# A second Strassen level over pairs of blocks, with PSUM banks copied to PSUM banks

## The chip, the core and the metric

The kernel runs on one core of a Trainium2 chip. A core has a matrix engine (TensorE, PE in the profile, with its weight loads as PEld), three other compute engines (VectorE = DVE, ScalarE = ACT, GpSimd = POOL), a queue of DMA issues on SyncE (SP), another one on GpSimd, and 16 DMA engines that serve both queues. Operands lie in SBUF, TensorE writes its products to one of eight PSUM banks of 128 x 512 fp32 numbers. Each engine takes its instructions in order; between engines semaphores make one wait for another. The metric is the device time of one execution in microseconds (us), as the median over runs.

## The reference

```python
x = A_x                                        # 1 x 2048 x 640
g = sigmoid((x * gate_w).sum(-1, keepdims=True))
a = real part of DFT over the sequence of the DFT over the hidden axis of x
b = (gelu(x @ w_gate) * (x @ w_up)) @ w_down   # F = 1728 hidden features
return g * a + (1 - g) * b
```

Everything is fp32. The change touches only `x @ w_gate` and `x @ w_up` and what feeds them.

## The kernel before

**Numbers.** fp32 products are made of three matmuls in a faster fp32 form (`mm3`, lines 84 to 87): each operand is split into a high part (a ScalarE copy, `high`, line 74) and a low part (a VectorE subtraction, `low`, line 77), and high x high, high x low and low x high are added up in one PSUM bank. So each operand of TensorE costs one ScalarE and one VectorE instruction, unless the split is already there.

**Stages.** First a prologue loads x and computes the first block of hidden features and the 64 that remain at the end; then twelve chunks compute gate and up for 128 features each (f = 1 to 12), from about 48 to 348 us; then come the down product (from 348 to about 500 us), the DFT over the sequence, and the last stage. The hidden values go to DRAM (`hA`, `hT`, by GpSimd's queue) and come back for the down product.

**A chunk.** For each of two token pairs (tp = 0, 1; 1024 tokens each) `gate_up` takes the weights as a 2 x 2 matrix A (gate and up by the two halves of inner blocks 0 to 3) and the tokens as a 2 x 2 matrix B, and uses the seven products of the Strassen-Winograd scheme: A11·B11, S1·T1, S2·T2, A12·B21, S3·T3, S4·B22, A22·T4. Each product is two `mm3` (two inner blocks i); the fifth inner block is added with `g5`, `u5` and `D`. That makes 18 `mm3`, 54 matmuls, per chunk and token pair, and 108 matmuls per chunk. Intermediate sums stay in the banks X, Z and V, and ScalarE copies X to SBUF as s1 and s2 on the way (L131 of the profile).

**Weights.** `load_w(f)` loads the two raw tiles wa and wb of chunk f, makes the sums S1 to S4 (`ws`) and the difference D (`wd`) on VectorE, and splits all of them. It is called a whole chunk ahead. Its raw tiles, parts and most other tiles of 4 KB per partition share one pool of 48 slots (tag "s4"); a new tile waits until the slot's former tile has been read for the last time. At the end of each chunk stand the sums of the down weights or up weights for later stages (`sum_wd`, `sum_wu`, lines 344 to 366: two loads, four VectorE sums, a store; for three of the up weights also negations `un` on ScalarE) and two of sixteen pieces of the gate's row sum (`load_z`, lines 386 to 391: a load, a multiply by the gate's weights and a reduction on VectorE).

**What sets the order.** In the prologue and from the down product on, the order of the engines is that of the code. In the chunks in between it is a scheduler's: it decides from priorities and from when operands are ready which instruction an engine takes next. Each engine then keeps to that list on the chip. The rows of such lists are shown below, with their line in the kernel; the last number behind an underscore only tells tiles apart.

## Time and profile before

| | |
|---|---|
| median of 3 runs | 1032.38 us (1030.0 to 1032.62) |
| the profiled execution | 1031.27 us, its span on the core 1029.5 us |
| TensorE busy | 1023.9 us, 99%, 4530 matmuls recorded |
| VectorE busy | 770.6 us, 75%, 1030 instructions |
| ScalarE busy | 449.6 us, 44%, 570 instructions |
| GpSimd busy | 132.2 us, 13% |
| read from and written to HBM | 169.21 MB, 63.98 MB |

The span runs from the first to the last instruction on the core; the execution's own time also has what lies around it. A matmul's row shows 0.39 us, yet the next one starts 0.23 us after it, because matmuls are pipelined: for TensorE, distances between starts tell the cost. Nearly all of a VectorE or ScalarE instruction's time is its own. In rows of waits, the three numbers are the us in total, how often, and the longest.

### The profile page before, as it was taken

How to read it: one execution, taken by the hardware profiler on the slowest of the kernel's cores; microseconds unless marked ns; L12 is line 12 of the kernel's file. 1: busy time of each engine (PE TensorE's matmuls, PEld its weight loads, DVE VectorE, ACT ScalarE, POOL GpSimd, SP SyncE). 2: the span in 40 equal slices, each digit the busy share in tenths (PEclk: the TensorE clock that was granted, in tenths of full speed). 3: DMA queues.
4: the chain of work that ended last, by engine and by line, in shares of the span. 5: the costliest groups of instructions: out<-in, count | busy, mean ns of one | idle time of the engine just before them, and what ended most of it. 6: DMA issues, size and time to landing. Idle time of an engine off the chain costs nothing.

```text
span 1029.5 us, 12790 instructions
## 1 busy us (share of the span) xinstructions
PE 1023.9 (99%) x4530; PEld 846.2 (82%) x4530; DVE 770.6 (75%) x1030; ACT 449.6 (44%) x570; POOL 132.2 (13%) x237
## 2 busy tenths in 40 slices
PE   9999999999999999999999999999999999999998
PEld 7888888888888888888888888888888888888887
DVE  6998675767654967986798975796678769697775
ACT  5453334343523546556345443343344344365430
POOL 0012121212121200100010011002000200021013
PEclk9999999999999999999999999999999999999999
DMA  8246644746446997878866577557656878897748
GB/s 299 74 153 219 221 169 160 239 160 240 154 148 215 381 346 242 276 253 287 288 216 206 209 224 280 178 198 245 257 177 217 273 275 278 288 328 212 283 94 133
DMA packets 78609, 234.05 MB, mean 227 GB/s; under 512 B 10096, under 2 KB 18320, under 8 KB 78544
## 3 DMA queue, kind: packets, MB, share of 16 engines
q1 hardware_dynamic: 57968, 169.31, 48.6%
q0 software_dynamic: 20432, 63.73, 18.4%
q8 instruction: 35, 0.57, 0.2%
q14 instruction: 30, 0.25, 0.1%
q10 hardware_dynamic: 144, 0.20, 0.1%
HBM read 169.21 MB, written 63.98 MB: 227 GB/s over the span
## 4 chain that ended last, share of the span: by engine, by line
PE 98%; DMA 1%; DVE 0%; ACT 0%; issue 0%; SPq 0%; ACTq 0%
PE pX L85 8%; PE pX L86 8%; PE pX L87 8%; PE pZ L86 5%; PE pZ L85 5%; PE pZ L87 5%; PE pV L86 3%; PE pV L85 3%; PE pV L87 3%; PE pL L85 3%; PE pL L87 3%; PE pL L86 3%; PE pY L87 1%; PE pY L85 1%; PE pR L87 1%; PE pR L85 1%
## 5 line engine op out<-in xcount | busy, mean ns | idle before, releaser
L74 ACT ACTIVATE ch<-csa 128x1024 fp32r<-128x1024 f32 x32 | 34.0, 1063 | 88.4 <-DVE csa L436 53.4
L131 ACT ACTIVATE s<-pX 128x512 f32<-128x512 f32 x64 | 37.8, 596 | 77.2 <-PE pX L87 69.2
L74 ACT ACTIVATE ch<-cra 128x1024 fp32r<-128x1024 f32 x32 | 33.9, 1058 | 47.4 <-PE pL L86 21.6
L77 DVE TENSOR_TENSOR cl<-crb,ch 128x1024 fp32r<-128x1024 f32 x32 | 39.1, 1221 | 17.0 <-ACT ch L74 9.7
L77 DVE TENSOR_TENSOR cl<-cra,ch 128x1024 fp32r<-128x1024 f32 x32 | 39.1, 1222 | 15.5 <-ACT ch L74 15.1
L86 PE MATMUL pL<-cl,xah 128*128 128x512 f32 x128 | 49.8, 389 | 0.0
L87 PE MATMUL pL<-ch,xal 128*128 128x512 f32 x128 | 49.8, 389 | 0.0
L85 PE MATMUL pL<-ch,xah 128*128 128x512 f32 x128 | 49.3, 389 | 0.0
L226 POOL DMA_DIRECT2D hA<-s x48 | 26.1, 544 | 177.0 <-DVE s L313 170.6
L303 DVE TENSOR_TENSOR s<-s,pV 128x512 f32<-128x512 f32 x24 | 16.3, 683 | 41.8 <-PE pV L87 17.6
L77 DVE TENSOR_TENSOR cl<-csb,ch 128x1024 fp32r<-128x1024 f32 x32 | 39.2, 1224 | 6.3 <-ACT ch L74 4.7
L74 ACT ACTIVATE ch<-crb 128x1024 fp32r<-128x1024 f32 x32 | 33.8, 1055 | 21.0 <-DVE cl L77 7.8
L77 DVE TENSOR_TENSOR cl<-csa,ch 128x1024 fp32r<-128x1024 f32 x32 | 39.1, 1221 | 4.0 <-ACT ch L74 3.3
L74 ACT ACTIVATE ch<-csb 128x1024 fp32r<-128x1024 f32 x32 | 33.9, 1059 | 11.9 <-PE pL L86 6.9
L77 DVE TENSOR_TENSOR kl<-kw,kh 128x1024 fp32r<-128x1024 f32 (+1 forms) x26 | 31.4, 1208 | 10.0 <-ACT kh L74 10.0
L74 ACT ACTIVATE kh<-kw 128x1024 fp32r<-128x1024 f32 (+1 forms) x26 | 27.3, 1048 | 11.6 <-DMA kw<-wsd 7.3
L312 ACT ACTIVATE s<-s 128x512 f32<-128x512 f32 x24 | 15.2, 633 | 38.8 <-DVE s L311 38.8
L788 POOL DMA_DIRECT2D uA<-s x16 | 8.7, 542 | 159.3 <-DVE s L834 152.5
L87 PEld LDWEIGHTS pL<-ch,xal 128*128 128x128 f32 x128 | 24.0, 188 | 5.0
L86 PEld LDWEIGHTS pL<-cl,xah 128*128 128x128 f32 x128 | 24.0, 188 | 5.0
L85 PEld LDWEIGHTS pL<-ch,xah 128*128 128x128 f32 x128 | 24.0, 188 | 5.0
L226 POOL DMA_DIRECT2D hT<-s x48 | 26.0, 543 | 14.9 <-DVE s L317 3.9
(3584 smaller groups left out, 3332.6 us busy)
## 6 DMA issues: line engine op xcount, KB each, us to landing
cra<-in_ct SPq DMA_DIRECT2D x64, 512.0 KB, 3.9
crb<-in_ct SPq DMA_DIRECT2D x64, 512.0 KB, 4.8
hA<-s POOLq DMA_DIRECT2D x48, 256.0 KB, 4.7
hT<-s POOLq DMA_DIRECT2D x48, 256.0 KB, 4.8
kr<-hA SPq DMA_DIRECT2D x24, 512.0 KB, 7.8
kr<-hT SPq DMA_DIRECT2D x24, 512.0 KB, 6.5
ux<-uA SPq DMA_DIRECT2D x24, 512.0 KB, 5.5
ux<-uT SPq DMA_DIRECT2D x16, 512.0 KB, 7.1
```

The costliest lines, as they stand in the source:

```text
L74: nc.scalar.activation(hi, raw, AF.Copy)
L77: nc.vector.tensor_tensor(lo, raw, hi.bitcast(F32), op=ALU.subtract)
L85: nc.tensor.matmul(ps, lh, rh, start=first, stop=False, skip_group_check=True)
L86: nc.tensor.matmul(ps, lh, rl, start=False, stop=False, skip_group_check=True)
L87: nc.tensor.matmul(ps, ll, rh, start=False, stop=last, skip_group_check=True)
L131: nc.scalar.activation(m, src, AF.Copy)
L226: nc.gpsimd.dma_start(to[:, i], src)
L303: tt(s1, s1, V, op=ALU.add)
L312: nc.scalar.activation(s2, s2, AF.Gelu_apprx_tanh)
L788: nc.gpsimd.dma_start(to[:, i], src)
```

## The change

Chunks 1 and 2 stay as they are. Chunks 3 to 12 are taken in five pairs (p = 1 to 5, f = 2p + 1 and 2p + 2). In a pair, A11·B11 for the two chunks and the two token pairs is itself a 2 x 2 by 2 x 2 product: rows are the two chunks, the inner dimension the two inner blocks, columns the two token pairs. So is A12·B21. `pair_first` computes each of the two (J = 1 for A11·B11, J = 2 for A12·B21) by a second level of the same scheme, 7 `mm3` in place of 8. Their weight operands are the parts of `pair_parts`: the blocks themselves (`ve`, `vq`) and four sums (`vs`, split to `vh` and `vl`). Their token operands are blocks that are there already, and the cross sums of both token pairs.

**Seeds.** In the scheme one product belongs to several outputs. Where a chain of sums in a bank must go on in two directions, `seed` copies the bank to another bank by ScalarE (six per pair: pv00, px00, pv01, px01, pv10, px10), and TensorE goes on adding to both. The products sv and sx are copied to SBUF and added by VectorE. All eight banks are in use then.

**Cross sums.** `cross_sums(J)` makes them once, during chunks 1 and 2, from a second load of x: VectorE sums, splits, and eight GpSimd stores to a DRAM tile `xtd`. One of them (`t3`) is split in place over a block of x that is no longer read. Because the 48 slots are full, the others are loaded again in each pair by `load_cross` (six loads of 512 KB: xx21, xx11, xx22, xx12, xx24, xx14), into slots that the pair before frees.

**Weights.** In place of `load_w`, the two raw tiles of a pair are loaded during the pair before (for the first pair in chunk 2, step 3), and `pair_parts` and `chain_parts` make the parts: the blocks 4 to 7 (`wp`, 512 wide) are split by `chain_parts`, the first four (`ve`) by `pair_parts`. `chain` then does the other products of a chunk, in four steps.

**Other work.** The down and up weights' sums follow one another after each chunk from chunk 3 on (`extras`), with two z pieces after each while there are some left, which is in pairs 1 to 4. A z piece is one fused instruction and a read of its sum (both shown as ISA). The last sum (`d5`) and the rows of the gate come at the end of pair 5.

TensorE has 4509 matmuls in place of 4539, VectorE 1101 rows in place of 1032, ScalarE 630 in place of 572, SP's queue 432 rows in place of 398.

```diff
+    xtd = {J: dram.tile([P, 3, 2, T], F32, tag=f"xtd{J}", name=f"xtd{J}") for J in (1, 2)}
...
+    def chain_parts(f, raw):
+        ra, rb = raw
+        sm, *c = wchunk(f"ws{f}")
+        g01, g23, u23 = ra[:, 0:2], ra[:, 2:4], ra[:, 5:7]
+        tt(sm[:, 0:2], rb, u23, op=ALU.add)
+        tt(sm[:, 4:6], g01, rb, op=ALU.subtract)
+        tt(sm[:, 2:4], sm[:, 0:2], g01, op=ALU.subtract)
+        tt(sm[:, 6:8], g23, sm[:, 2:4], op=ALU.subtract)
+        a, d = slot(F32R, [P, 2, 4, P], f"wp{f}"), wsmall(F32R, f"wd{f}")
+        split(*c, sm)
+        split(a[:, 0], a[:, 1], ra[:, 4:8])
+        tt(rb[:, 1], ra[:, 4], ra[:, 7], op=ALU.subtract)
+        split(d[:, 0], d[:, 1], rb[:, 1])
...
+    def pair_parts(p, r0, r1):
+        a, b = (r[:, 0:4].rearrange("q (j k) c -> q k j c", j=2) for r in (r0, r1))
+        sm = slot(F32, [P, 4, 2, P], f"vs{p}")
+        h, l = slot(F32R, [P, 4, 2, P], f"vh{p}"), slot(F32R, [P, 4, 2, P], f"vl{p}")
+        e, q = slot(F32R, [P, 2, 4, P], f"ve{p}"), pool.tile([P, 2, 2, P], F32R, tag="m", name=f"vq{p}", bufs=12)
+        tt(sm[:, 0], b[:, 0], b[:, 1], op=ALU.add)
+        tt(sm[:, 2], a[:, 0], b[:, 0], op=ALU.subtract)
+        tt(sm[:, 1], sm[:, 0], a[:, 0], op=ALU.subtract)
+        tt(sm[:, 3], a[:, 1], sm[:, 1], op=ALU.subtract)
+        split(h, l, sm)
+        split(e[:, 0], e[:, 1], r0[:, 0:4])
+        split(q[:, 0], q[:, 1], b[:, 1])
...
+    def cross_sums(J):
+        r = [pair(F32, f"xc{J}{q}") for q in range(2)]
+        for q in range(2):
+            nc.sync.dma_start(r[q], xt[2 * q, 2 * J - 2 : 2 * J].rearrange("d p c -> p d c"))
+        b11, b21, b12, b22 = r[0][:, 0], r[0][:, 1], r[1][:, 0], r[1][:, 1]
+        u, v = pair(F32, f"xu{J}"), pair(F32, f"xv{J}")
+        tt(u[:, 0], b12, b11, op=ALU.subtract)
+        tt(u[:, 1], b22, u[:, 0], op=ALU.subtract)
+        tt(v[:, 1], b21, u[:, 1], op=ALU.subtract)
+        tt(v[:, 0], b22, b12, op=ALU.subtract)
+        h, l = hl(f"xU{J}")
+        split(h, l, u)
+        h4, l4 = mtile(F32R, f"xh{J}"), mtile(F32R, f"xl{J}")
+        split(h4, l4, v[:, 1])
+        for k, (a, b) in enumerate(((h, h4), (l, l4))):
+            nc.gpsimd.dma_start(xtd[J][:, 0:2, k], a.bitcast(F32))
+            nc.gpsimd.dma_start(xtd[J][:, 2, k], b.bitcast(F32))
+        return v[:, 0]
+    tcross = {}
+    def load_cross(J, i):
+        tcross[J, i] = slot(F32R, [P, 2, T], f"xx{J}{i}")
+        nc.sync.dma_start(tcross[J, i].bitcast(F32), xtd[J][:, {1: 0, 2: 1, 4: 2}[i]])
...
+    def seed(ps, name):
+        b = bank(name)
+        nc.scalar.activation(b, ps, AF.Copy)
+        return b
+    def pair_first(p, WP, W):
+        b = {J: {"b11": at(Bs[0][J, 1], 0), "b21": at(Bs[0][J, 1], 1), "b22": at(Bs[1][J, 1], 1), "t3": at(Bs[1][J, 1], 0)} for J in (1, 2)}
+        for J in (1, 2):
+            for i in (1, 2, 4):
+                c = tcross.pop((J, i))
+                b[J][f"t{i}"] = c[:, 0], c[:, 1]
+        def m(ps, J, w, x, first=False):
+            mm3(ps, WP[J][w], b[J][x], first, True)
+        def fifth(ps, f, q):
+            mm3(ps, W[f]["g5"], at(Bs[q][5], 0), False, True)
+        def gated(s1, *more):
+            for v in more:
+                tt(s1, s1, v, op=ALU.add)
+            nc.scalar.activation(s1, s1, AF.Gelu_apprx_tanh)
+        va, xa_, ve, xe = (bank(f"p{n}{p}") for n in ("va", "xa", "ve", "xe"))
+        X, s1 = {}, {}
+        m(va, 2, "a11", "b11", True)
+        v00 = seed(va, f"pv00{p}")
+        m(xa_, 1, "a11", "b11", True)
+        X[0, 0] = seed(xa_, f"px00{p}")
+        m(ve, 2, "s1", "t1", True)
+        sv = copy(ve, f"sv{p}")
+        m(v00, 2, "a12", "b21")
+        m(xe, 1, "s1", "t1", True)
+        sx = copy(xe, f"sx{p}")
+        m(va, 2, "s2", "t2")
+        v01 = seed(va, f"pv01{p}")
+        m(X[0, 0], 1, "a12", "b21")
+        s1[0, 0] = copy(X[0, 0], f"s100{p}")
+        m(xa_, 1, "s2", "t2")
+        X[0, 1] = seed(xa_, f"px01{p}")
+        fifth(v00, 0, 0)
+        gated(s1[0, 0], v00)
+        m(v01, 2, "s4", "b22")
+        m(va, 2, "s3", "t3")
+        v10 = seed(va, f"pv10{p}")
+        m(X[0, 1], 1, "s4", "b22")
+        tt(X[0, 1], X[0, 1], sx, op=ALU.add)
+        s1[0, 1] = copy(X[0, 1], f"s101{p}")
+        m(xa_, 1, "s3", "t3")
+        X[1, 0] = seed(xa_, f"px10{p}")
+        tt(xa_, xa_, sx, op=ALU.add)
+        X[1, 1] = xa_
+        s1[1, 1] = copy(xa_, f"s111{p}")
+        fifth(v01, 0, 1)
+        gated(s1[0, 1], v01, sv)
+        m(v10, 2, "a22", "t4")
+        fifth(v10, 1, 0)
+        m(X[1, 0], 1, "a22", "t4")
+        s1[1, 0] = copy(X[1, 0], f"s110{p}")
+        gated(s1[1, 0], v10)
+        fifth(va, 1, 1)
+        gated(s1[1, 1], va, sv)
+        return X, s1
...
-        nc.vector.tensor_tensor(r, r, gwb, op=ALU.mult)
-        nc.vector.tensor_reduce(z[:, sb : sb + 1], r, axis=mybir.AxisListType.X, op=ALU.add)
+        nc.vector.tensor_tensor_reduce(r, r, gwb, 1.0, 0.0, ALU.mult, ALU.add, z[:, sb : sb + 1])
...
-    for f in range(1, NF):
-        nxt = load_w(f + 1) if f + 1 < NF else None
+    sq = [lambda k=k: sum_wd(k) for k in range(NK)]
+    for p in range(ND):
+        sq.insert(2 * p + 1, lambda p=p: sum_wu(p))
+    def extras(n):
+        sq.pop(0)()
+        for _ in range(n):
+            load_z(zq.pop(0))
+    t3 = {}
+    W2 = load_w(2)
+    for f in (1, 2):
         s5 = pair(F32, f"s5{f}")
         work = [gate_up(f, W, Bs[tp], tp, s5[:, tp]) for tp in range(2)]
         for step in range(7):
             for w in work:
                 next(w)
-            if f == NF - 1:
-                if step == 1:
-                    split_k(0)
-                if step >= 4:
-                    load_k(step - 3)
-        if f % 2:
-            sum_wd(f // 2)
-        elif f <= 2 * ND:
-            sum_wu(f // 2 - 1)
-        if f == NF - 2:
-            gate_rows()
-            gm = [gate_tile(gmd, tp, f"gm{tp}") for tp in range(2)]
-            load_k(0)
-        for _ in range(2):
-            if f > 1 and zq:
-                load_z(zq.pop(0))
-        W = nxt
+            if (f, step) in ((1, 4), (2, 1)):
+                J = 2 if f == 1 else 1
+                t3[J] = cross_sums(J)
+            if f == 2 and step == 3:
+                raws = load_raw(3), load_raw(4)
+        W = W2
+    WP = pair_parts(1, raws[0][0], raws[1][0])
+    W0_ = chain_parts(3, raws[0])
+    for J in (2, 1):
+        for i in (1, 2):
+            load_cross(J, i)
+    for J in (1, 2):
+        split(Bs[1][J, 1][0][:, 0], Bs[1][J, 1][1][:, 0], t3[J])
+    for p in range(1, NK):
+        f = 2 * p + 1
+        for J in (2, 1):
+            load_cross(J, 4)
+        Ws = [W0_, chain_parts(f + 1, raws[1])]
+        X, s1 = pair_first(p, WP, Ws)
+        for i in range(2):
+            s5 = pair(F32, f"s5{f + i}")
+            work = [chain(f + i, Ws[i], Bs[tp], tp, s5[:, tp], X[i, tp], s1[i, tp]) for tp in range(2)]
+            for step in range(4):
+                for w in work:
+                    next(w)
+                if p < NK - 1:
+                    if (i, step) == (0, 2):
+                        raws = load_raw(f + 2), load_raw(f + 3)
+                    if (i, step) == (1, 0):
+                        WP = pair_parts(p + 1, raws[0][0], raws[1][0])
+                    if (i, step) == (1, 1):
+                        for J in (2, 1):
+                            load_cross(J, 1)
+                    if (i, step) == (1, 2):
+                        W0_ = chain_parts(f + 2, raws[0])
+                        for J in (2, 1):
+                            load_cross(J, 2)
+                elif i == 1:
+                    if step == 0:
+                        split_k(0)
+                    if step >= 1:
+                        load_k(step)
+            extras(2 if zq else 0)
+            if (p, i) == (NK - 1, 0):
+                sq.pop(0)()
+                gate_rows()
+                gm = [gate_tile(gmd, tp, f"gm{tp}") for tp in range(2)]
+                load_k(0)
```

VectorE at the end of chunk 2, before: s12_0 is s1 of chunk 2 and token pair 0, s21_1 is s2 of chunk 1, s51 and s52 are s5; d1s is a sum of down weights.

```order
L324 TENSOR_TENSOR s12_0_751<-s12_0_751,pX2_0_742 128x512
L317 TENSOR_TENSOR s21_1_620<-s22_1_798,s21_1_620 128x512
L319 TENSOR_TENSOR s51_563<-s22_1_798,s51_563 128x512
L327 TENSOR_TENSOR s52_741<-s12_0_751,s51_563 128x512
L324 TENSOR_TENSOR s12_1_762<-s12_1_762,pX2_1_753 128x512
L327 TENSOR_TENSOR s52_741<-s12_1_762,s51_563 128x512
L339 TENSOR_TENSOR d1s_1086<-da1_1083,dr1_1082 128x256
```

And now, with the pair's weight sums `vs1` and the low parts `vl1`, `ve1` between the chunk's last rows:

```order
L397 TENSOR_TENSOR s12_0_744<-s12_0_744,pX2_0_735 128x512
L390 TENSOR_TENSOR s21_1_622<-s22_1_813,s21_1_622 128x512
L392 TENSOR_TENSOR s51_565<-s22_1_813,s51_565 128x512
L400 TENSOR_TENSOR s52_734<-s12_0_744,s51_565 128x512
L397 TENSOR_TENSOR s12_1_755<-s12_1_755,pX2_1_746 128x512
L262 TENSOR_TENSOR vs1_919<-wa3_837,vs1_919 128x256
L400 TENSOR_TENSOR s52_734<-s12_1_755,s51_565 128x512
L77 TENSOR_TENSOR vl1_921<-vs1_919,vh1_920 128x1024
L77 TENSOR_TENSOR ve1_922<-wa3_837,ve1_922 128x512
L237 TENSOR_TENSOR ws3r_934<-wb3_838,wa3_837 128x256
L238 TENSOR_TENSOR ws3r_934<-wa3_837,wb3_838 128x256
```

The last sum of vs1 (L262) and the low parts that the next pair reads stand behind the two reads of the banks pX2 (L397), where before no weight of the next chunk was left to make.

ScalarE at the same place, before (from the last activations of chunk 2 on to the copies of chunk 3):

```order
L74 ACTIVATE ws4h_922<-ws4r_921 128x1024
L312 ACTIVATE s22_0_790<-s22_0_790 128x512
L312 ACTIVATE s22_1_798<-s22_1_798 128x512
L131 ACTIVATE s13_0_945<-pX3_0_936 128x512
L131 ACTIVATE s13_1_956<-pX3_1_947 128x512
L296 ACTIVATE s53_935<-pZ3_0_937 128x512
```

And now:

```order
L385 ACTIVATE s22_1_813<-s22_1_813 128x512
L74 ACTIVATE vh1_920<-vs1_919 128x1024
L74 ACTIVATE ve1_922<-wa3_837 128x512
L410 ACTIVATE pv001_989<-pva1_982 128x512
L74 ACTIVATE wd3_942<-wb3_838 128x128
L74 ACTIVATE ws3h_935<-ws3r_934 128x1024
L410 ACTIVATE px001_994<-pxa1_983 128x512
L74 ACTIVATE wp3_941<-wa3_837 128x512
L132 ACTIVATE sv1_999<-pve1_984 128x512
```

High parts of the pair's weights stand ahead of the first seed; the high part of ws3 stands ahead of the seed px00.

TensorE's first matmuls of the second pair, now (va, xa, ve, xe are banks of that pair; a bank named pv00 or px00 is a seed of pva or pxa):

```order
L85 MATMUL pva2_1393<-x021h_151,ve2_1231 128x512
L86 MATMUL pva2_1393<-x021l_152,ve2_1231 128x512
L87 MATMUL pva2_1393<-x021h_151,ve2_1231 128x512
L85 MATMUL pxa2_1394<-x011h_148,ve2_1231 128x512
L86 MATMUL pxa2_1394<-x011l_149,ve2_1231 128x512
L87 MATMUL pxa2_1394<-x011h_148,ve2_1231 128x512
L85 MATMUL pv002_1400<-x021h_151,ve2_1231 128x512
L85 MATMUL pve2_1395<-xx21_1259,vh2_1229 128x512
L86 MATMUL pve2_1395<-xx21_1259,vh2_1229 128x512
L87 MATMUL pve2_1395<-xx21_1259,vl2_1230 128x512
L86 MATMUL pv002_1400<-x021l_152,ve2_1231 128x512
L87 MATMUL pv002_1400<-x021h_151,ve2_1231 128x512
```

One matmul on the seed pv00 (L85) comes four rows after the one that closes pva (the first L87); the rest of it follows three rows later. The first product with xx22 is row 636, with xx12 642, with xx24 663, with xx14 668.

SP's queue at that place, before (the loads during chunks 4 and 5):

```order
L357 DMA ua1_1277<-in_wu 128x256
L203 DMA wb6_1297<-in_wf 128x256
L356 DMA ur1_1276<-in_wu 128x1024
L389 DMA xz4_1286<-in_xz 128x640
L389 DMA xz5_1290<-in_xz 128x640
```

And now, where the second pair starts between the rows ur0 and xz2:

```order
L296 DMA xx21_1259<-xtd2_127 128x1024
L296 DMA xx11_1261<-xtd1_126 128x1024
L548 DMA ua0_1358<-in_wu 128x256
L296 DMA xx22_1293<-xtd2_127 128x1024
L296 DMA xx12_1295<-xtd1_126 128x1024
L547 DMA ur0_1357<-in_wu 128x1024
L580 DMA xz2_1367<-in_xz 128x640
L580 DMA xz3_1370<-in_xz 128x640
L296 DMA xx24_1373<-xtd2_127 128x1024
L296 DMA xx14_1375<-xtd1_126 128x1024
```

The loads of xx22 and xx12 take slots that the matmuls 607 and 608 (products with x122 in chunk 4) read last, and those of xx24 and xx14 the ones that matmuls 638 and 641 (in the second pair) read last; ur0, xz2 and xz3 stand between them.

ScalarE in the fourth pair, now:

```order
L410 ACTIVATE pv004_2230<-pva4_2223 128x512
L410 ACTIVATE px004_2235<-pxa4_2224 128x512
L132 ACTIVATE sv4_2240<-pve4_2225 128x512
L132 ACTIVATE sx4_2248<-pxe4_2226 128x512
L553 ACTIVATE un2_2183<-ur2_2179 128x256 x2
L553 ACTIVATE un2_2183<-ur2_2179 128x128
L553 ACTIVATE un2_2183<-ur2_2179 128x384
L410 ACTIVATE pv014_2253<-pva4_2223 128x512
L132 ACTIVATE s1004_2258<-px004_2235 128x512
```

The negations of the up weights (L553), which need the load of ur2, stand between the copies sv, sx and the seed pv01. Before, they stood (as L362) around the first of a chunk's copies s2.

More of the change, by code (lines that the diff above doesn't have):

```diff
@@ L223, in load_w, with load_raw @@
         return W
+    def load_raw(f):
+        ra, rb = slot(F32, [P, 8, P], f"wa{f}"), wsmall(F32, f"wb{f}")
+        nc.sync.dma_start(ra, wf[f - 1, :, :8])
+        nc.sync.dma_start(rb, wf[f - 1, :, 8:])
+        return ra, rb
+    def chain_parts(f, raw):
[11 more added lines that the diff above has]
+        split(d[:, 0], d[:, 1], rb[:, 1])
+        W = {"D": (d[:, 0], d[:, 1]), "g5": (a[:, 0, 0], a[:, 1, 0]), "u5": (a[:, 0, 3], a[:, 1, 3])}
+        for i in range(2):
+            W["A22", i] = a[:, 0, 1 + i], a[:, 1, 1 + i]
+            for k in range(4):
+                W[f"S{k + 1}", i] = at(c, 2 * k + i)
+        return W
@@ new lines, in chain, with prod @@
+    def chain(f, W, B, tp, s5, X, s1):
+        n = f"{f}_{tp}"
+        Z = bank(f"pZ{n}")
+        x1, x2 = at(B[5], 0), at(B[5], 1)
+        k, second = divmod(f - 1, 2)
+        def prod(ps, a, b, first):
+            for i in range(2):
+                mm3(ps, W[a, i], at(B[b], i), first and i == 0, True)
+        prod(Z, "S1", "T1", True)
+        mm3(Z, W["u5"], x2, False, True)
+        nc.scalar.activation(s5, Z, AF.Copy)
+        yield
+        prod(X, "S2", "T2", False)
+        s2 = copy(X, f"s2{n}")
+        yield
+        prod(X, "S3", "T3", False)
+        tt(s5, s5, X, op=ALU.add)
+        yield
+        prod(Z, "S4", (2, 2), False)
+        mm3(Z, W["D"], x2, False, True)
+        tt(s2, s2, Z, op=ALU.add)
+        last_products(X, W, B, tp, k, second, s1, s2, s5, prod)
+        yield
```

27 lines of the change are left out of this document (added).

## The prediction

> **What bounds the kernel now.** I read the totals first, then TensorE's waits, then the windows around the change, and last the timeline at one chunk boundary.
>
> ```profile
> span 1029.5 us, 12790 instructions
> ...
> PE 1023.9 (99%) x4530; PEld 846.2 (82%) x4530; DVE 770.6 (75%) x1030; ACT 449.6 (44%) x570; POOL 132.2 (13%) x237
> ...
> PE   9999999999999999999999999999999999999998
> ```
>
> ```profile
> PE pwarm L656 <- DVE warm L613: 1.2, 1, 1.2
> PE pm L263 <- ACT x011h L74: 0.5, 1, 0.5
> PE kX L85 <- ACT ks L131: 0.3, 1, 0.3
> ```
>
> The page's totals give TensorE 1023.9 us of the 1029.5, in every one of the 40 slices 90% or more except the last. The three wait rows are TensorE's complete list: 2.0 us, and none of it in the gate and up chunks. So the time before is the number of matmuls times their cadence. A matmul taken out is worth one slot, and a wait put in front of TensorE costs its full length.
>
> ```profile
> 98.00:100.00 2.00, 2.00 (x10) 1.68 (x9) 1.97 (x4) 0.95 (x2) 1.83 (x4) 1.00 0.97 352
> 100.00:102.00 2.00, 2.00 (x10) 1.65 (x10) 1.97 (x5) 0.60 (x1) 0.66 (x2) 1.00 1.04 415
> 60.00:100.00 40.00, 40.00 (x177) 32.86 (x176) 34.16 (x63) 17.62 (x29) 9.09 (x17) 1.00 0.58 190
> 100.00:130.00 30.00, 30.00 (x134) 24.82 (x134) 18.25 (x33) 10.21 (x16) 5.00 (x10) 1.00 0.66 237
> ```
>
> These are stretches of time with the busy time of TensorE, weight load, VectorE, ScalarE and GpSimd, the granted clock, the DMA share and GB/s. TensorE is full throughout. Around the boundary of chunks 2 and 3 (96.2 us) VectorE is full as well (34.16 of 40 us; 1.97 of 2) and the 16 DMA engines are saturated (0.97 and 1.04). New work that TensorE needs early in a pair therefore meets two engines without room.
>
> **The gain: 30 matmuls.** Timeline, at the boundary where the first pair will stand:
>
> ```profile
> 95.97 0.39 PE L87 MATMUL pX<-x15h,wa2l 128*128 128x512 f32 x1
> ...
> 96.20 0.39 PE L85 MATMUL pX<-x011h,wa3h 128*128 128x512 f32 x1
> ...
> 97.33 0.39 PE L87 MATMUL pX<-x011h,wa3l 128*128 128x512 f32 x1
> ...
> 97.76 0.60 ACT L131 ACTIVATE s<-pX 128x512 f32<-128x512 f32 x1 [2.72 <-PE pX L87]
> ...
> 97.89 0.68 DVE L327 TENSOR_TENSOR s<-s,s 128x512 f32<-128x512 f32 x1
> ...
> 98.50 0.68 DVE L324 TENSOR_TENSOR s<-s,pX 128x512 f32<-128x512 f32 x1
> ...
> 98.69 0.39 PE L87 MATMUL pX<-x111h,wa3l 128*128 128x512 f32 x1
> ```
>
> From 96.20 to 98.69 lie 11 slots, 0.2264 us each. A pair of blocks had 16 three-matmul products A11·B11 and A12·B21 and will have 14, so 2 × 3 matmuls less in each of 5 pairs: 30 × 0.2264 = **−6.8 us**, if TensorE stays gapless. Everything else is what the change puts in front of TensorE. The added VectorE and ScalarE instructions (some 70 and 60) cost nothing as totals, since both have idle time over a whole pair (18.25 and 10.21 busy of 30); what counts is when the operands come.
>
> **The first pair.** Before, wa3's parts were split a whole chunk ahead. Now vs1's last row (L262), its split vh1 and the split ve1 stand on VectorE and ScalarE behind VectorE's read (L397) of chunk 2's last product, matmul row 410; the first matmul of the pair needs ve1. I price the chain from slot 411, the 96.20 of before.
>
> ```profile
> 90.00 1.06 ACT L74 ACTIVATE ws4h<-ws4r 128x1024 fp32r<-128x1024 f32 x1
> ...
> 90.22 1.22 DVE L77 TENSOR_TENSOR wa4l<-wa4r,wa4h 128x1024 fp32r<-128x1024 f32 x1
> ...
> 91.35 0.68 DVE L311 TENSOR_TENSOR s<-s,pZ 128x512 f32<-128x512 f32 x1
> ...
> 100.15 0.42 DVE L340 TENSOR_TENSOR d1s<-dr,da 128x256 f32<-128x256 f32 x1
> ...
> 100.49 0.42 DVE L341 TENSOR_TENSOR d1s<-d1s,dr 128x256 f32<-128x256 f32 x1
> ...
> 4.12 0.64 ACT x011h L74
> ```
>
> VectorE's read starts between +0.2 us (matmul 410 at 95.97 plus the 0.43 that the copy at 97.76 needs after its matmul at 97.33) and +2.3 (where the backlog put this same read before, at 98.50). VectorE has lost the 1024-wide splits of the next weights here, and has cross sums instead, so I take +0.95. Then 0.60 for the read (97.89 to 98.50 is such a step), 0.42 for L262, 1.06 for vh, 0.64 for ve's high part (x011h's row, the nearest of that size): slot 411 starts at +3.7, a **3.7 us wait**. VectorE goes on with vl (1.13 until the next may start, 90.22 to 91.35) and ve's low part; matmul 413 needs it, at +5.0 where +4.2 would do: 0.8. Seed px00 stands on ScalarE behind ws3's 1024-wide high split, and that behind five small VectorE sums (0.34 apart, 100.15 to 100.49): matmul 420 is 1.5 late. Four smaller ones, read from the order in the same way (seeds pv00, pv01 and pv10, and wp3's low part): 0.15, 0.2, 0.5, 0.1. Sum **+7.0**. With the read at +0.2 and the four gone it is 5.3; with the read at +2.3 and the four doubled, 9.3.
>
> **Seeds in pairs 2 to 5.** Bank-to-bank copies on ScalarE are not in this trace; the bank-to-SBUF copy (0.60, starting 0.43 after its last matmul) is nearest. Matmul 627 continues the seed of a bank closed by matmul 623, with three matmuls between. The seed is ready 0.43 + 0.60 + 0.06 = 1.09 after 623 starts, and 627 is due after 4 × 0.2264 = 0.91: 0.2 per pair, **+0.8**. Half of the copy's time would make it nothing, double 3.1. [...]
>
> **Cross loads.** xx22 and xx12 (512 KB each) are queued on SP in the pair before, but take slots that matmuls 607 and 608 of chunk 4 free, so they issue 2.75 us ahead of the pair's first slot. They are needed 3.4 and 4.75 after it. That leaves 6.3 and 7.3 us of latency (0.2 of it from the seed wait). What 512 KB took:
>
> ```profile
> xz<-in_xz SPq DMA_DIRECT2D x16, 320.0 KB, 5.3
> dr<-in_wd SPq DMA_DIRECT2D x5, 512.0 KB, 3.8
> ur<-in_wu SPq DMA_DIRECT2D x4, 512.0 KB, 3.8
> ...
> wa4r<-in_wf SPq DMA_DIRECT2D x1, 512.0 KB, 6.8
> ...
> wa11r<-in_wf SPq DMA_DIRECT2D x1, 512.0 KB, 7.3
> ```
>
> Two cross loads, ur and the outgoing hA/hT stores start together here, so I take wa4r's 6.8 rather than dr's 3.8: 0.5 late; ends 0 and 1.0. xx24 and xx14 come later: in pairs 2 and 3 they issue 4.5 us into the pair, behind ur and two xz pieces on SP, and are due at 9.5, which the waits above make 10.2. 5.7 against 3.8 to 7.3: 0 to 1.6, I take 0.6.
>
> **VectorE in pairs 2 and 3.** There, wp6 (matmuls 675 to 681) waits behind the gated add, two z pieces and the sums of ws6.
>
> ```profile
> L390 DVE TENSOR_TENSOR xz<-xz,gwb 128x640 f32<-128x640 f32 x16 | 13.1, 819 | 13.2 <-DMA xz<-in_xz 13.2
> L391 DVE TENSOR_REDUCE z<-xz 128x1 f32<-128x640 f32 x16 | 13.0, 812 | 0.1
> ...
> L362 ACT ACTIVATE un<-ur 128x256 f32<-128x256 f32 x6 | 2.5, 409 | 0.0
> L362 ACT ACTIVATE un<-ur 128x384 f32<-128x384 f32 x3 | 1.5, 513 | 0.0
> ...
> L362 ACT ACTIVATE un<-ur 128x128 f32<-128x128 f32 x3 | 0.9, 301 | 0.0
> ```
>
> A fused z piece is not in the trace: at least the multiply's 0.82, at most both rows, 1.63. Between these, wp6's low part is 0.25 to 1.85 late if nothing else held TensorE; waits that came earlier in the pair absorb part, and I take 0.6. Together with the loads, 0.5 + 0.6 + 0.6 = 1.7 in each of two pairs: **+3.4** (0 to 6).
>
> **ScalarE in pairs 4 and 5.** The four negations un (2 × 0.41 + 0.30 + 0.51 = 1.63) now stand ahead of seed pv01 on ScalarE, and wait for ur, which issues 2.2 us before the pair. Landing in 3.8 to 7.3, they end between 3.2 and 6.7 after the pair's start; the seed could begin at 4.3 and its matmul is due at 6.1, so 0 to 1.2, I take 0.6. With the 0.5 of xx22: 1.1 in each, **+2.2** (0 to 4). Here xx24 and xx14 are needed 1 us later and are left at nothing.
>
> **Costed at nothing.** The cross sums (4 loads, 8 GpSimd stores, VectorE and ScalarE steps in chunks 1 and 2) lie between steps that TensorE doesn't wait for. The weights of each pair's second block (ws4, wd4, wp4) stand in the first half of the pair, a chunk ahead of their products. The down weights' sums and their store move to the end of the chunks: the store of d5 is read some 34 us into the next stage, and the first split of that stage comes, by my count of VectorE's rows, 0.4 us ahead of its matmul; if that cover is gone it costs a few tenths.
>
> **Sum.** −6.8 + 7.0 + 0.8 + 3.4 + 2.2 = **+6.6**. The profiled execution took 1031.27 (its span 1029.5), 1.1 under the median of 1032.38. 1031.27 + 6.6 = 1037.9: **1038 us**. A difference below 0.3% (3.1 us) can hardly be told from none here: faster is below 1029.3, slower above 1035.5.
>
> **Rivals.**
> - The other side, one mechanism: at the first pair the waits overlap instead of adding up. VectorE reads product 410 at +0.2, and the splits behind vh and ve are done while TensorE already stands, so that only the first wait (2.9) remains and the later ones, as the slack of whole pairs suggests, vanish: −6.8 + 2.9 + 0.8 = −3.1, 1028.2. It decides where all waits together stay below 4.8. Against it: vl, ve_l, ws3 are in series on engines that take them in order.
> - The saving is eaten up but no more: the loads and the seeds are hidden (512 KB in 3.8) and the first pair costs its 5.3 to 7: 1030 to 1032, and with half of the 5.6 of the later pairs, up to 1035. For it speaks that dr and ur mostly landed in 3.8.
> - Loads late in every pair: DMA at 0.97 to 1.04 after each boundary, 7.3 per load; 10 in place of 5.6: 1042.3, with the first pair at its upper end 1044.6.
> - The clock falls back during the first wait.
>
> ```profile
> 1.20 3.17 PE L656 MATMUL pwarm<-warm 128*128 128x512 bf16 x7 [1.20 <-DVE warm L613]
> ...
> 5.42 0.63 PE L263 MATMUL pg<-x011h,w0h 128*128 128x512 f32 x1
> 5.84 0.63 PE L263 MATMUL pu<-x011h,w0h 128*128 128x512 f32 x1
> ...
> 7.23 0.40 PE L267 MATMUL pm<-x011h,w0l 128*128 128x512 f32 x1
> ```
>
> At the start, after TensorE stood still, 7 matmuls took 3.17 (1.6 more than at 0.2264), and the next five to 7.0 another 1.0. Such a restart inside the pair costs up to 2.6: 1040.5. [...]
>
> **How the numbers follow.** The forecast's case (1035.5 to 1041) 0.42; loads late 0.15; the clock 0.08; together slower 0.65. Eaten up but no more: 0.22. Faster 0.13. The range leaves out the far end of the faster case and of the late loads: 1029 to 1046.
>
> **What would show it.** TensorE's rows 4509. Its list of waits gets a first entry of 3 to 4 us on a high split (L74) at about 96 us, then some of 0.5 to 1.5 on VectorE's low splits and on seeds (L410); at about 151, 200, 250 and 298 us (47.5 us of slots a pair, and the waits above) waits below 1 us on xx loads or seeds; ScalarE's seeds 0.5 to 0.6 long. Without those, I am wrong towards faster. A granted clock below 1.00 in the window 100 to 104 shows the clock's rival. I would be wrong to the slow side if stores and loads of the boundary push xx22 beyond 8 us, or if the fused z piece takes longer than both rows it replaces.

## The result, and the profile after

The changed kernel takes 1080.59 us (median of 4 runs, 1078.95 to 1081.44) against 1031.41 us before: ratio 1.0475, 95% interval 1.0455 to 1.0496. The forecast was 1038, with a range of 1029 to 1046. The sign was right, the size was not: 49 us more instead of 7.

Page of the changed kernel:

```profile
span 1077.1 us, 12983 instructions
...
PE 1031.4 (96%) x4500; PEld 843.4 (78%) x4500; DVE 794.7 (74%) x1099; ACT 479.3 (44%) x631; POOL 137.5 (13%) x245
...
PEclk9999998989999979999999999999999999999999
```

TensorE is no longer gapless (96%), and it is busy for 7.5 us longer although it has 30 matmuls less: in three of the 40 slices (seventh, ninth and fifteenth: pairs 2 and 3, and the entry of the down product) the clock row falls below 9. Its longest waits, and one short one:

```profile
PE kX L86 <- DVE kb0010l L77: 12.5, 1, 12.5
PE pv L85 <- DMA xx<-xtd: 7.1, 2, 5.8
PE pv L85 <- ACT wd L74: 6.6, 2, 4.1
PE px L85 <- ACT s L132: 5.0, 4, 1.7
PE pva L85 <- ACT ve L74: 3.4, 1, 3.4
PE pv L85 <- ACT pv L410: 3.1, 2, 1.6
PE px L85 <- DMA xx<-xtd: 1.3, 2, 0.6
...
PE pva L87 <- DVE ve L77: 0.6, 1, 0.6
```

Before, the whole list was 2.0 us long; here it is 41. Two things need care. First, `pv <- ACT wd` is matmul row 663 of pair 2 and its fellow in pair 4, the first product with xx24 (in pairs 3 and 5 the same product stands under `pv <- DMA xx`):

```profile
161.19 0.58 ACT L410 ACTIVATE pv<-pva 128x512 f32<-128x512 f32 x1
...
165.95 0.77 PE L85 MATMUL pv<-xx,vq 128*128 128x512 f32 x1 [4.14 <-ACT wd L74]
```

It needs the seed pv10, whose copy was done at 161.8, and the load, which landed at 165.81; ScalarE's wd only happened to finish nearby. Second, a wait costs more than its row shows, by 0.2 to 0.3 for the restart, and by matmuls at half the clock when it was long:

```profile
162.00:166.00 4.00, 0.05 (x1) 0.08 (x1) 3.19 (x10) 0.70 (x3) 0.00 (x0) 0.93 1.03 419
166.00:170.00 4.00, 3.94 (x9) 2.67 (x10) 3.56 (x6) 2.41 (x4) 0.00 (x0) 0.50 0.95 324
```

In the stretch after the wait at row 663 of pair 2 the granted clock is 0.50 and 9 matmuls fall in 4 us, where some 18 would fit at 0.2265 us.

So I add up, for each place, by how much the distances between the starts of neighbouring matmuls in the timeline exceed 0.2265 us (from 90 to 400 us):

| place | us |
|---|---|
| entry of the down product (kb0010's low part) | 12.7 |
| products with xx24 and xx14 (pairs 2 to 5: 4.8, 5.9, 3.4, 2.3) | 16.5 |
| S3·T3 of a pair's second chunk, behind the copy s2 (pairs 1 to 4: 1.5, 1.8, 1.4, 0.9) | 5.7 |
| first pair: ve, its low part, seed px00 | 4.8 |
| seed pv01 behind the negations (pairs 4 and 5) | 3.5 |
| matmuls at half the clock, after four of these waits (1.6, 2.8, 2.6, 1.6) | 8.6 |
| seeds (0.25 a pair), restarts and other small ones, the rest | 3.3 |
| sum | 55.1 |

55.1 − 6.8 = 48.3 us; the spans differ by 47.6. What remained to be found out was why each place waits, and whether the second level is worth anything without them.

**The entry of the down product.** VectorE, then SyncE's waits:

```profile
380.33 0.69 DVE L519 TENSOR_TENSOR s<-s,s 128x512 f32<-128x512 f32 x1
390.60 0.43 DVE L530 TENSOR_TENSOR d5s<-da,dr 128x256 f32<-128x256 f32 x1 [9.57 <-DMA dr<-in_wd]
...
393.08 1.22 DVE L77 TENSOR_TENSOR kb0010l<-kr,kb0010h 128x1024 fp32r<-128x1024 f32 x1
```

```profile
SPq L574 <- DMA gmd<-gr: 16.4, 1, 16.4
```

VectorE stands 9.6 us at the first sum of d5, whose load has not landed, and kb0010's low part is in its list behind the sums of d5. The gate rows are loaded after the first chunk of pair 5, not at the pair's end. SyncE's queue stood 16.4 us at their loads gm, until 361.7, because they wait for a store of the same rows; all loads of the down product and d5's came behind them, within 20 us. The load of d5 was issued at 376.9 and landed at 390.5: 13.6 us, in the middle of that bunch.

**The middle of a pair.** DMA issues of the window 152 to 168 us in pair 2:

```profile
hT<-s POOLq DMA_DIRECT2D x4, 256.0 KB, 8.4
xx<-xtd SPq DMA_DIRECT2D x2, 512.0 KB, 10.3
xz<-in_xz SPq DMA_DIRECT2D x2, 320.0 KB, 7.5
hA<-s POOLq DMA_DIRECT2D x2, 256.0 KB, 8.9
wsu<-u0s POOLq DMA_DIRECT2D x1, 512.0 KB, 8.3
```

xx24 and xx14 are issued at 156.4 and 157.1, 4.6 and 5.2 us after the pair's start (151.8), and land after 9.4 and 11.3 (10.3 is the middle of the two); over pairs 2 to 5 it is 9.4 to 12.5. The loads xx22 and xx12, issued at the head of the same bunch, landed after 4.2 to 6.4.

**S3·T3 in a pair's second chunk.** VectorE, ScalarE and TensorE in pair 1:

```profile
135.07 0.42 DVE L530 TENSOR_TENSOR d0s<-da,dr 128x256 f32<-128x256 f32 x1 [1.64 <-DMA da<-in_wd]
...
138.77 0.42 DVE L262 TENSOR_TENSOR vs<-wa,vs 128x256 f32<-128x256 f32 x1
...
139.22 1.06 ACT L74 ACTIVATE vh<-vs 128x1024 fp32r<-128x1024 f32 x1 [1.81 <-DVE vs L262]
...
140.81 0.50 PE L85 MATMUL px<-xT03h,ws4h 128*128 128x512 f32 x1 [1.32 <-ACT s L132]
```

VectorE stands at the load da of a down sum, then makes that sum and one z piece between the sums vs of the next pair; ScalarE has vh, which needs vs, ahead of the copy s2, and TensorE may go on in the copied bank only behind that copy. In pairs 1 to 4 VectorE stood 1.64, 2.00, 1.59 and 1.11 us at da, and TensorE lost 1.5, 1.8, 1.4 and 0.9 behind it.

### The profile page after: what moved, and what is told of

It reads as the page before. It is cut to its first block, busy times and chain, and to the rows that moved or that the text cites. A ratio compares the mean times of both kernels' runs of the same rounds, so it can differ in the third digit from the quotient of the medians.

```text
span 1077.1 us, 12983 instructions
## 1 busy us (share of the span) xinstructions
PE 1031.4 (96%) x4500; PEld 843.4 (78%) x4500; DVE 794.7 (74%) x1099; ACT 479.3 (44%) x631; POOL 137.5 (13%) x245
## 4 chain that ended last, share of the span: by engine, by line
PE 86%; DMA 9%; DVE 3%; issue 1%; ACT 1%; SPq 0%; POOL 0%; ACTq 0%; DVEq 0%; POOLq 0%
PE pZ L85 4%; PE pZ L86 4%; PE pZ L87 4%; PE pX L85 3%; PE pX L87 3%; PE pX L86 3%; DMA xx<-xtd 3%; PE pL L87 3%; PE pL L85 3%; PE pL L86 3%; PE px L85 2%; PE px L87 2%; PE px L86 2%; PE pV L87 2%; PE pV L85 2%; PE pV L86 2%
## 5 line engine op out<-in xcount | busy, mean ns | idle before, releaser
L87 PE MATMUL pL<-ch,xal 128*128 128x512 f32 x128 | 49.8, 389 | 0.0
L85 PE MATMUL pL<-ch,xah 128*128 128x512 f32 x128 | 49.3, 389 | 0.0
L77 DVE TENSOR_TENSOR kl<-kw,kh 128x1024 fp32r<-128x1024 f32 (+1 forms) x26 | 31.5, 1210 | 11.3 <-ACT kh L74 11.3
L505 ACT ACTIVATE s<-s 128x512 f32<-128x512 f32 x20 | 12.6, 632 | 53.7 <-DVE s L499 53.7
L1019 POOL DMA_DIRECT2D uA<-s x16 | 8.7, 543 | 158.5 <-DVE s L1065 151.7
L625 DVE TENSOR_TENSOR csa<-cra 128x512 f32<-128x512 f32 x32 | 22.0, 687 | 8.4 <-PE pL L86 6.5
L739 POOL DMA_DIRECT2D out<-ks x12 | 6.5, 543 | 168.2 <-DVE ks L738 167.6
L87 PEld LDWEIGHTS pL<-ch,xal 128*128 128x128 f32 x128 | 24.0, 188 | 5.0
L85 PEld LDWEIGHTS pL<-ch,xah 128*128 128x128 f32 x128 | 24.0, 188 | 5.0
```

The source lines that it names most:

```text
L77: nc.vector.tensor_tensor(lo, raw, hi.bitcast(F32), op=ALU.subtract)
L85: nc.tensor.matmul(ps, lh, rh, start=first, stop=False, skip_group_check=True)
L87: nc.tensor.matmul(ps, ll, rh, start=False, stop=last, skip_group_check=True)
L505: nc.scalar.activation(s2, s2, AF.Gelu_apprx_tanh)
L625: tt(s1[:, 0], r1[:, 1], r1[:, 0], op=ALU.subtract)
L739: nc.gpsimd.dma_start(out[2 * tp + t, e], src)
```

## The experiments

Nothing is left out of the computation in any of these kernels; they move work. Each is an edit of the changed kernel. Ratios are to the kernel before, run beside it; e1 to e6 have two runs each, e7 to e11 have eleven or twelve.

**Entry of the down product, by VectorE's order (e1).**

```diff
-            extras(2 if zq else 0)
+            if sq:
+                extras(2 if zq else 0)
             if (p, i) == (NK - 1, 0):
                 sq.pop(0)()
+                sq.pop(0)()
                 gate_rows()
```

> Edit: the last down sum d5 is made in pair 5 after its first chunk, with d4 and u4, and not at its end. Theory (VectorE's order): the 12.5 us wait at the entry of the down product is VectorE standing at d5's first sum, which waits for the load dr5; kb0010's low part is only queued behind it. Then the wait falls to 0 to 2 us, the half-clock matmuls after it go, and the time falls by 11 to 15 us, to 1066 to 1070. Rival (SyncE's queue): the loads of the down stage itself are late because SP stands at the gate rows; then a wait of more than 7 us stays there, now on a kr or kw load, and the time falls by less than 6 us.

**The same, by SyncE's queue (e2).**

```diff
-                gm = [gate_tile(gmd, tp, f"gm{tp}") for tp in range(2)]
                 load_k(0)
+    gm = [gate_tile(gmd, tp, f"gm{tp}") for tp in range(2)]
     order = ctx.enter_context(ExitStack())
```

> Edit: the two gate-row loads gm are issued behind the first four sets of down loads; d5 stays at the end. SyncE's queue theory: with gm out of the way the down loads and dr5 are issued up to 20 us earlier, dr5 lands before VectorE reaches d5, the 12.5 us wait falls below 2 us and the time by 11 to 15 us. VectorE's order theory with loads limited by free slots: dr5 takes a slot that a matmul of chunk 12 frees, so moving gm hardly helps; the wait stays above 8 us and the time falls by less than 5 us.

e1: 1069.01 us, ratio 1.0374 (1.0344 to 1.0405). e2: 1066.33 us, ratio 1.0348 (1.0303 to 1.0394). In e1 three short waits stay there:

```profile
381.10 0.50 PE L85 MATMUL kL<-kb0000h,kh 128*128 128x512 f32 x1 [1.13 <-DVE s L499]
383.08 0.50 PE L85 MATMUL kL<-kb0000h,kh 128*128 128x512 f32 x1 [0.33 <-DVE s L516]
387.28 0.50 PE L86 MATMUL kX<-kb0010l,kh 128*128 128x512 f32 x1 [1.43 <-DVE kb0010l L77]
```

In e2 TensorE has no wait between 350 and 400 us: d5's load is issued at 370.4 and lands at 378.3, 12 us earlier than in the changed kernel. Both rivals fall: the wait needs both things, a late load and an instruction that VectorE must pass on its way, and taking either away takes 10 (e1: excess 3.9 instead of 14.3) or 14 us (e2: nothing left).

**The middle of a pair (e3, e5).** e3 moves sums and z pieces behind a chain's first step, e5 the z pieces alone:

```diff
                 if p < NK - 1:
+                    if step == 0:
+                        extras(2 if zq else 0)       # e3
+                        for _ in range(2):           # e5
+                            load_z(zq.pop(0))        # e5
                     if (i, step) == (0, 2):
...
-            extras(2 if zq else 0)
+            if p == NK - 1:
+                extras(0)                            # e3; e5: extras(0) for every p
```

> Edit: in pairs 1 to 4 the weight sums and the z pieces stand behind the first step of a chunk's chain instead of at the chunk's end, so their loads (ur or dr, two xz) and stores leave the start of the next pair. Bunched-DMA theory: xx24 and xx14 landed in 10.3 us because these transfers shared the engines at 410 to 426 GB/s; without them they land in 4 to 7 us, the waits on them (16 us over four pairs) fall below 4 in sum, the waits of seed pv01 behind un (3.5) go, half-clock stretches after them go (6 to 7), total 20 to 28 us less: 1053 to 1061. Rival: the four cross loads and the hidden-value stores saturate the engines alone; then 3 to 4 us of wait stay in each pair and the time falls by less than 10 us.

> Edit: only the two z pieces go behind the first step of a chunk's chain; the weight sums stay at the chunk's end. The loads xx24 and xx14 of pairs 2 and 3 may then take slots that are free some 2 us earlier, and 640 KB less (1.6 us at 410 GB/s) go out ahead of them. If both the late issue and the shared bandwidth make them late, the waits of 4.1 and 5.8 us there fall by 3 to 4 us; if only the issue counts, by 2; if the weight sums' own transfers (ur and its store, 1 MB) are what they wait for, by less than 1. In pairs 4 and 5 the negations stay ahead of seed pv01 and so do the waits of 1.5 to 1.6. In all 4 to 10 us less than the changed kernel's 1080.6.

e3: 1065.57 us, ratio 1.0341 (1.0311 to 1.0371), between what the two theories said. In pairs 2 and 3 not one wait is left, the excess there is 0.5 and 0.4 us in 50 instead of 9.9 and 8.8, and the copies behind vh are gone as well. But pairs 4 and 5 have a new wait, at their first matmul:

```profile
251.55 0.80 PE L85 MATMUL pva<-x021h,ve 128*128 128x512 f32 x1 [4.27 <-ACT ve L74]
...
309.03 0.79 PE L85 MATMUL pva<-x021h,ve 128*128 128x512 f32 x1 [5.80 <-ACT ve L74]
```

```profile
249.92 1.06 ACT L74 ACTIVATE vh<-vs 128x1024 fp32r<-128x1024 f32 x1 [1.79 <-DVE vs L262]
```

There the sums of u2 and u3, with their negations, and a z piece now stand on VectorE ahead of the last sum of the next pair's vs: moved to a place where they delay the weights. What made xx24 late can be read in the same run. In 158 to 162 us the DMA engines are as full as they were (a share of 1.03 in the changed kernel too), and TensorE doesn't wait:

```profile
158.00:162.00 4.00, 4.00 (x19) 3.34 (x18) 3.42 (x7) 3.88 (x7) 1.08 (x2) 1.00 1.03 412
```

SyncE issued all six cross loads by 151.7, half a microsecond after the pair's start, against 156.4 and 157.1 for the last two in the changed kernel. There the queue held these two until matmuls of the pair itself had finished; in e3, without ur, its sums and two xz ahead of them, it didn't have to. Measured from the pair's start, xx24 was issued 5.3 us earlier, and it landed after 6.2 instead of 9.4. So the late issue is the larger part, and the latency among the other transfers the smaller one.

e5: 1070.96 us, ratio 1.0385 (1.0366 to 1.0404), as expected in sum. In pairs 2 and 3 xx24 is issued 1.7 us earlier, and the waits there shrink from 4.1 to 3.1 and from 5.8 to 3.3: on average what the issue gained, but not in each. Two other places tell more. The wait at seed pv01 in pair 4 did not stay but grew from 1.5 to 2.4, since ur landed later. And S3·T3 still waits 0.3 to 1.0 us, instead of 0.8 to 1.7: without the z piece, the down sum and its load still stand ahead of vs. e3, which moves the sums too, takes this wait away.

**The first pair (e4, e6).** e4 loads the raw weights two steps earlier and makes the pair's sums before chunk 2 ends; e6 makes the parts of the chain earlier too, and splits wp ahead of ws:

```diff
-            if f == 2 and step == 3:
+            if f == 2 and step == 1:
                 raws = load_raw(3), load_raw(4)
+            if f == 2 and step == 5:                 # e6: 3
+                WP = pair_parts(1, raws[0][0], raws[1][0])
+            if f == 2 and step == 4:                 # e6 only
+                W0_ = chain_parts(3, raws[0])
...
-    WP = pair_parts(1, raws[0][0], raws[1][0])
-    W0_ = chain_parts(3, raws[0])                    # e6 only
```

> Edit: the raw weights of the first pair are loaded two steps earlier in chunk 2 and its sums made before the chunk ends, so that vs1's last sum and the splits vh1, ve1 stand ahead of VectorE's reads of chunk 2's last products. Theory: the first pair's waits (3.6 + 0.8) and the half-clock matmuls after them (2.6) go, 5 to 7 us less: 1074 to 1076. Rival: at the same place the cross loads xx11, xx12 or seeds behind ws3's split are late next; then 2 us or less are gained.

> Edit: for the first pair, the raw weights, the pair's sums and the parts of the chain are all made earlier in chunk 2, and in every chunk wp is split ahead of ws. In e4 the first wait had only gone from ve to wp (2.8 + 0.6). If the weights alone hold the first pair, all waits there (4.0 in the changed kernel, 4.4 in e4) fall below 1 and the half-clock stretch behind them goes: 5 to 7 us less than 1080.6. If the next operand is late there too (xx11, xx12, a seed), 2 to 4 us of wait stay at the first pair.

e4: 1081.20 us, ratio 1.0493 (1.0462 to 1.0523): nothing gained, and not for the rival's reason. The first wait fell from 3.4 to 0.4, and the next part of the same weights took its place:

```profile
96.52 0.50 PE L85 MATMUL pva<-x021h,ve 128*128 128x512 f32 x1 [0.39 <-ACT ve L74]
97.86 0.50 PE L87 MATMUL pva<-x021h,ve 128*128 128x512 f32 x1 [0.61 <-DVE ve L77]
103.48 0.50 PE L85 MATMUL pv<-x05h,wp 128*128 128x512 f32 x1 [2.79 <-ACT wp L74]
```

e6: 1078.94 us, ratio 1.0463 (1.0444 to 1.0482). The first pair has two waits left (0.6 on xx11, 0.8 on VectorE), the excess from 90 to 150 us falls from 8.9 to 4.3, no matmul there runs at half the clock. Yet the time falls by 1.6 us only, which is within the noise of the two runs: the wait for xx24 in pair 5, 1.4 before, is 3.1, and 13 matmuls behind it are 0.43 us apart (excess 300 to 350 us: 9.0 instead of 5.8). Why it grew is not shown.

**All together (e7), and what was left of the first pair (e8 to e11).** e7 takes e2, e6 (with `chain_parts` one step later), and e3 with the up weights' sums first and both behind the making of the next pair's parts:

```diff
-        sq.insert(2 * p + 1, lambda p=p: sum_wu(p))
+        sq.insert(2 * p, lambda p=p: sum_wu(p))
...
                         for J in (2, 1):
                             load_cross(J, 2)
+                    if step == 0:
+                        extras(2 if zq else 0)
```

> All edits together: first pair's weights early and wp first, sums (up weights first) and z pieces in mid-chunk behind the making of the next pair's parts, gate rows loaded after the down loads. If the waits and the half clock after them are all that the change costs, what stays is the 30 matmuls (-6.8 us) and the small seed waits (0.2 to 0.3 a pair): 1025 to 1028 us, faster than before by 3 to 6 us. If the second level itself costs (bank copies, more matmuls on ScalarE's path, DMA), it stays above 1031.

1033.66 us, ratio 1.0022 (1.0013 to 1.0031): 47 us of the 49 are gone, yet 1025 to 1028 was not reached. It is above 1031, but not because the level itself costs in every pair. From 150 to 350 us, with four pairs, the excess is 3.4 us; the first pair alone has 6.3 in 90 to 150:

```profile
110.69 0.79 PE L85 MATMUL px<-xx,vq 128*128 128x512 f32 x1 [2.46 <-ACT px L410]
```

e8 makes the sums of the second chunk's ws and wd after `pair_first`, e9 also loads xx21, xx11, xx22, xx12 in this order, and e10 makes those sums after the chain's first step:

```diff
-        Ws = [W0_, chain_parts(f + 1, raws[1])]
+        W1_, rest = chain_parts(f + 1, raws[1])      # rest(): ws and wd
+        Ws = [W0_, W1_]
         X, s1 = pair_first(p, WP, Ws)
+        rest()                                       # e8, e9; e10: at (i, step) == (0, 0)
...
-    for J in (2, 1):
-        for i in (1, 2):
+    for i in (1, 2):                                 # e9, e10
+        for J in (2, 1):
             load_cross(J, i)
```

> As e7, and the sums of a pair's second chunk (ws, wd) are made behind pair_first instead of ahead of it, so that on ScalarE their splits stand behind the seeds. In e7 the first pair still lost 6.2 us: 0.9 on xx11, and 2.5 where seed px10 stood behind the splits wd4 and ws4, with 1.2 of half clock behind it. If that order is the cause, the first pair loses 2 us or less and the time falls from 1033.7 to 1028 to 1031. If the first pair is held by the loads xx24 and xx14 as such, the 2.5 us stay and so does the time.

> As e8, and in the first pair the four cross loads are issued in the order of their use (xx21, xx11, xx22, xx12). If xx11 was late only because xx22 took the earlier slot, its wait of 0.9 (1.1 with the restart) goes: 1 us less than e8. If the four loads together are the limit, the wait goes to xx22 and nothing is gained.

> As e9, and the sums and splits of the second chunk's ws and wd are made only after the first step of the pair's chain. In e9 the first pair still lost 3.9 us, of it 1.7 where seed pv10 stood behind wd4's split, which waits for VectorE, and 0.8 where an addition waits for a copy of px00. If the place of that split is the cause, the 1.7 go: 1028.5 to 1029.5 us, 0.1 to 0.2% faster than before. If xx24's landing stands right behind it, less than 0.5 is gained.

e8: 1031.58 us, ratio 1.0007 (0.9998 to 1.0016); the first pair's excess is 4.1, not 2, with 1.5 now at seed pv10. e9: 1030.87 us, ratio 0.9998 (0.9989 to 1.0007); the wait on xx11 is gone, and 0.7 on a copy of px00 has come: 3.9. e10: 1033.18 us, ratio 1.0027 (1.0018 to 1.0036), not the 1028.5 to 1029.5 expected; the first pair is down to 2.7, and the old wait at the entry of the down product is back:

```profile
346.39 0.42 DVE L533 TENSOR_TENSOR d5s<-da,dr 128x256 f32<-128x256 f32 x1 [4.82 <-DMA dr<-in_wd]
...
349.00 1.22 DVE L77 TENSOR_TENSOR kb0010l<-kr,kb0010h 128x1024 fp32r<-128x1024 f32 x1
```

So with gm out of the way the load of d5 is only just in time or not; e2 had hidden that. e11 adds e1's edit:

```diff
             if (p, i) == (NK - 1, 0):
-                sq.pop(0)()
+                while sq:
+                    extras(0)
                 gate_rows()
```

> As e10, and d5's sum is made with the other last sums after the first chunk of pair 5 (the edit of e1). In e10 the first pair loses only 2.7 us, but VectorE stood again 4.8 us at d5's load at the entry of the down product (3.9 us of TensorE, 1.6 of half clock). If that is all that makes e10 slower than e9, 5 to 6 us go: 1027.5 to 1029 us, 0.15 to 0.3% faster than before, and the spread of the runs gets smaller. If the entry is held by the loads of hA as such, a wait of 2 us or more stays there.

1028.48 us (11 runs, 1027.53 to 1030.6), ratio 0.9981 (0.9972 to 0.9990): faster than before by 0.1 to 0.3%, and the fastest of all kernels here. Its waits, complete:

```profile
PE pva L85 <- DMA xx<-xtd: 1.6, 1, 1.6
PE pwarm L849 <- DVE warm L806: 1.2, 1, 1.2
PE pm L339 <- ACT x011h L74: 0.5, 1, 0.5
PE pv L85 <- ACT pv L413: 0.3, 1, 0.3
```

Of the 6.8 us, 4.4 are still given back in the chunks (2.9 in the first pair, 0.3 to 0.9 in each later one); by that sum the span would be 1029.5 − 6.8 + 4.4 = 1027.1, and it is 1026.2.

## Why the prediction was wrong

| step of the prediction | forecast | measured |
|---|---|---|
| 30 matmuls | −6.8 | −6.8 (e11's span agrees to 1 us) |
| first pair | +7.0 | 4.8, and 1.6 of half clock |
| seeds | +0.8 | about 1.0 |
| cross loads and VectorE, pairs 2 and 3 | +3.4 | 4.8 + 5.9, and 5.4 of half clock |
| pairs 4 and 5 | +2.2 | 3.4 + 2.3 at xx24 and xx14, 3.5 at seed pv01 |
| entry of the down product | 0 | 12.7, and 1.6 of half clock |
| copy s2 behind vh | not seen | 5.7 |

- **What bounds the kernel** was right: TensorE has no slack, and every wait came out in full.
- **The first pair** went as worked out: VectorE's read at 96.23, vh at 97.29, ve at 98.25, TensorE after a wait of 3.4 us where 3.7 was forecast. The 1.5 us at seed px00 shrank to 0.5, since the matmuls ahead of it ran at half the clock.
- **Cross loads** is the step that failed most: for xx24 and xx14, 0.6 in each of pairs 2 and 3 and nothing in pairs 4 and 5 were forecast; 16.5 us of waits came, and 5.4 of half clock behind them. The issue times were right (4.5 us into the pair forecast, 4.6 measured), and the latency was wrong. 3.8 to 7.3 were taken as its ends from single loads before; behind two more cross loads, ur, xz and the hidden values it was 9.4 to 12.5. The page of before had loads of the same size in a bunch:

```profile
kr<-hA SPq DMA_DIRECT2D x24, 512.0 KB, 7.8
```

7.8 us is their median there, and the longest took 16.1: the upper end for a load in a bunch stood in the trace, and I didn't use it. xx22 and xx12, where I expected 0.5 a pair, were never waited for.
- **Costed at nothing** is the step that failed next. I took the first split of the down product to be 0.4 us ahead of its matmul "by my count of VectorE's rows", a count in which d5's load had landed. I did look at where d5's store is read, but not at the load behind which VectorE would stand, nor at what holds SyncE's queue. The sentence "it costs a few tenths" had no bound from a row; the same kind of row (VectorE standing 6.3 us for un, at no cost) had been in front of me.
- **VectorE behind the z pieces** was not what held row 663, nor did row 675 wait: the fused piece takes 0.82 + 0.08 us, near the lower bound, and row 663 starts at 165.95, right behind xx24's landing at 165.81. The z pieces stood in the way in SyncE's queue, with their loads ahead of xx24 (e5).
- **Negations ahead of seed pv01**: the mechanism was right, 1.7 us each instead of 0.6 and beyond the 1.2 of the bound.
- **S3·T3**: in the second chunk of a pair ScalarE has vh ahead of the copy s2, and vh waits for VectorE's last sum of vs, which stood behind a z piece, a down sum and, above all, the load da of that sum. It is the pattern that I had priced at the pair's start, four more times, and that of d5 as well: an in-order engine standing at a load that nobody needs yet. I had only gone through ScalarE's list near the pair's beginnings.
- **The clock** had 8 chances in 100, an estimate of mine that no row of this case shows. It fell at every wait of about that length or more (27 of 27 from 3.1 us up), and the sign named for it came: 0.57 in the window 100 to 104. The size per wait, up to 2.6, was about right (1.6 to 2.8 with the restart).
- **The rivals**: "loads late in every pair" with 1042 to 1045 was the nearest, and right on its place. None had the entry of the down product. The range was built from upper ends of the places that I had priced; those costed at nothing and those not gone through had no end in it, and they made 26 of the 48 us: the entry (14.3), xx24 and xx14 in pairs 4 and 5 (5.7), and S3·T3 (5.7).

## What to carry to other kernels

Where the matrix engine has no gap, a change that saves matmuls lives or dies by what its new operands wait for: go through each engine's list once for the whole stretch, and at every place where an in-order engine or queue meets something that depends on a load, ask what stands behind it. Here a sum that is read only some 34 us into the next stage and a load of gate rows cost 14 us at a stage's entry, and moving work off a pair's start without looking at the next weights made new waits of 4 to 6. A single wait removed often shows the next one (e4, e10), so several edits have to be made before the gain can be seen; and when transfers are bunched, issue the one that is needed first earlier, and price it by loads that stood in a bunch before (here a median of 7.8 us, the longest 16.1), rather than by the latency of single loads (3.8 us, the median of dr and of ur before).

## What the runs showed of the hardware

**The clock after a wait.** In the changed kernel and e1 to e6, every one of the 27 waits of TensorE of 3.1 us and more was followed by matmuls 0.43 us apart, 5 to 13 of them within 8 us, 1.0 to 2.6 us in sum. Over 30 waits of 0.9 to 2.0 us had none that was not from another, longer one. Between, it went both ways: 2.49 and 2.95 without, 2.40 (e5) and 2.46 (e7) with, and 2.79 (e4) with a second wait of 0.6 close behind. Such a stretch is at about half speed: a granted clock of 0.50 (changed kernel, 166 to 170 us), and 0.43 us between matmuls instead of 0.2265. What decides between 2.4 and 3.1 us is not shown. For planning, 2.4 us, the shortest wait with such matmuls behind it, is the number that these runs give.

**Bank to bank.** A copy of 128 x 512 from one PSUM bank to another on ScalarE takes as long as one to SBUF:

```profile
L410 ACT ACTIVATE pv<-pva 128x512 f32<-128x512 f32 x15 | 8.7, 581 | 5.0 <-PE pva L87 4.8
...
L132 ACT ACTIVATE sv<-pve 128x512 f32<-128x512 f32 x5 | 3.0, 600 | 4.5 <-PE pve L87 4.5
```

0.58 against 0.60 us: the difference of 3% is too little to take away the 0.25 us a pair that the seeds cost, where only three matmuls cover one.

**What a removed wait is worth.** TensorE's wait rows sum up to 41 us less the 2 of before, the matmuls saved are 6.8, and the span grew by 47.6: so a good quarter of the loss (15 of 54 us) stands in no wait row, but in half-clock matmuls, restarts and waits too short for a row.
